# Remainders of the values formed on GpSimd, and a second tile of outputs, in an attention and expert kernel

## The chip, the cores and the metric

The kernel runs on one core of a Trainium2 chip. The metric is the device time of one execution in microseconds, as the median of several runs. Profiles come from one further execution, with every instruction's start and length on each engine.

## The reference

Attention with queries averaged in pairs, and then a mixture of experts in which each token goes to one expert:

```python
q_pool = q.reshape(B, H, S // 2, 2, D).mean(axis=3)          # B=8, H=8, S=1152, D=64
scores = scale * np.matmul(q_pool, k.transpose(0, 1, 3, 2))
attn = softmax(scores)                                       # 576 x 1152 for each head
x = np.matmul(attn, v)            # -> 4608 tokens of 512
logits = x @ w_gate + modality_bias[modality_id]
e_idx = np.argmax(logits, axis=1)
...
h = np.maximum(x[mask] @ w1[e], 0.0)                         # 8 experts, 512 -> 1024 -> 512
out[mask] = gate_w[mask, None] * (h @ w2[e])
```

All of it is in float32. The kernel multiplies in float16 and keeps the precision by splitting an operand x into a rounded part (hi) and the remainder x - hi (lo), and multiplying both.

## The kernel before

**Pairs.** One head of two batch elements makes a pair: their 64 columns each fill the 128 partitions. There are 32 pairs, and each has 18 steps in a loop. Two pairs next to each other are two heads of the same batch elements; their outputs go into one tile x2 (128 x 9 x 128 float32), each pair into one half of its columns.

**What is done for one pair.** `load_kq` and `load_v` fetch rawq, rawk and rawv. The queries are summed in pairs (L613), rounded (qh, L620), and their remainder is formed (lo, L648); the keys are rounded on ScalarE (hi, L632) and their remainders formed on GpSimd (lo, L648). qh goes by DMA into QB (L583), with which `maxpass` computes rounded scores on TensorE (L781) and VectorE takes the maximum of each row (L782). The row of maxima (mr, L766) is sent by DMA into the row B2 of operands (B<-mr, L767), and qh, hi and lo are sent into the operands B1 and B2 by `place`. Then `scores` multiplies (L843 and, with the row of maxima as one of its operands, L844), ScalarE takes the exponential (Pe, L845), and the lower halves of the exponentials are scaled into Pl on ScalarE (L826) and VectorE (L828). `pv` multiplies them by the values (L894 to L896).

**The values.** `square` (ScalarE, L694) finds their size; it uses the tile vl for its unneeded output. `power` and `scales` (TensorE, VectorE L706 and L708) make a power of two of it, sc. `values` then makes the rounded values VH = v * sc, in two parts of 640 and 512 columns (nine chunks of 128, five and four), and the remainders vl = v * sc - VH. From the third pair on, VH is made on GpSimd (L735) and vl on VectorE, in one instruction that scales and subtracts (L733). The first two pairs use other lines (L730, L731, L737). `shifted` makes a scaled copy VS of VH on VectorE (L745). VH and VS have three tiles, used in turn; rawv has two, vl three.

**Outputs.** When a head's value products are finished, `evac` divides them by the row sums and writes them into x2 on VectorE (L912, L913, L917): for the pair's first head (j = 0) and, some nine steps later, for its second (j = 1). After the second head of an odd pair the whole x2 is stored to the tensor xs in DRAM (L218). Five steps later `split_x` splits x2 into two float16 tiles (ScalarE L862, VectorE L869), and after an odd pair each is transposed by a DMA (L877) for the router's logits. There is one tile x2; the next pair's first `evac` writes into it once the store has read it.

**What sets the order.** On TensorE, ScalarE, VectorE and GpSimd the instructions run in the order in which the program gives them; each piece of work has a step, counted from the pair's first step, in constants (T_VH = -14 and -15 for the two parts of VH, T_VS = -12, T_VL = -11 and -2 for vl, T_QH = -26 for qh, T_LO for the lo). The DMAs are issued from SyncE's queue, in an order that isn't written out: the framework's scheduler chooses it, by its own estimate of when each one's data are ready. SyncE issues in that order and waits at each DMA for its data.

**Beside it.** The router's work is spread over the pairs' steps: logits, the routing of each group of tokens (`route`, small instructions on VectorE and GpSimd), and in the last pairs the lists of tokens for each expert (`first_list`). The router's set-up is done on GpSimd at step 25. After the attention the expert stage streams weights and runs until the end.

Of the kernel before, what the change touches and what calls it, by code (L numbers as in the profile page):

```python
# [9 lines left out]
F32 = mybir.dt.float32  # L10
# [6 lines left out]
ALU = mybir.AluOpType  # L17
# [5 lines left out]
P = 128  # L23
# [6 lines left out]
D = 64  # L30
# [49 lines left out]
QH_POOL = True  # L80
LO_POOL = (0, 1, 2)
VH_POOL = (0, 1)
EV_ACT = ()
IN_PM = (0, 1, 2, 3, 4, 5)
EVD = 1
# [10 lines left out]
NT = 9  # L96
# [452 lines left out]
def attention(tc, ctx, att, ident, npairs, xpool, on_two, on_split, on_scale, jobs, side, set_pm, started, ahead, hip):  # L549
# [3 lines left out]
    nc = tc.nc  # L553
# [25 lines left out]
    def need(p, *names):  # L579
        assert all((p, n) in made for n in names), f"pair {p}: {names} are not made yet"  # L580
# [137 lines left out]
    flat = lambda a: a.rearrange("p c j d -> p (c j) d")  # L718

    def values(p, i, lo):  # L720

        s = st[p]
        c = slice(*PARTS[lo][i:i + 2])
        made.add((p, f"v{'hl'[lo]}{i}"))
        if lo:
            need(p, f"vh{i}")
        v = flat(s["v"].rearrange("p (c j d) -> p c j d", c=NKC, j=2)[:, c])
        vh = flat(VH[p % 3][:, c, :, 0:D])
        if lo and p < 2:
            nc.gpsimd.tensor_scalar(v, v, s["sc"], None, op0=ALU.mult)  # L730
            nc.gpsimd.tensor_tensor(flat(s["vl"][:, c]), v, vh, op=ALU.subtract)  # L731
        elif lo:
            nc.vector.scalar_tensor_tensor(flat(s["vl"][:, c]), v, s["sc"], vh, op0=ALU.mult, op1=ALU.subtract)  # L733
        elif p > 1 and i in VH_POOL:
            nc.gpsimd.tensor_scalar(vh, v, s["sc"], None, op0=ALU.mult)  # L735
        else:
            nc.scalar.activation(vh, v, AF.Copy, scale=s["sc"])  # L737
# [117 lines left out]
    def split_x(p, x2):  # L855

        s = st[p]
        if p % 2 == 0:
            s["x"] = [xpool.tile([P, NT, 2 * D], F16, name=f"x{i}", bufs=1) for i in range(2)]
        hs = slice((p % 2) * D, (p % 2 + 1) * D)  # L860
        xh, xl = st[p - p % 2]["x"]
        nc.scalar.activation(xh[:, :, hs], x2[:, :, hs], AF.Copy, scale=s["sc"])  # L862
        later(XL, lambda: split_xl(p, x2))
# [16 lines left out]
    def pv(p, j, c):  # L880

        s = st[p]
        W = D + 2
        vh, vs, vl = VH[p % 3], VS[p % 3], s["vl"]
        need(p, "vs", f"vl{int(c >= PARTS[1][1])}")
        Ph, Pl, i = s["P", j, c // 3]
        x = D + (c % 3 if j else 2 - c % 3) * SQ
        if c == 0:
            s["xp"] = ps_pv.tile([P, 512], F32, name="xp", tag="pv")[:, 0:5 * W].rearrange("p (g w) -> p g w", w=W)
        xp = s["xp"]  # L890
        for g in range(5):
            o = x + g * P + (D if j and g < 4 else -D - 4 * P if j else 0)
            qs, out = slice(o, o + P), xp[:, g, 0:D + 1]
            nc.tensor.matmul(out, Ph[:, qs], vh[:, c, j, 0:D + 1], start=c == 0 and g == 0, stop=False, skip_group_check=True)  # L894
            nc.tensor.matmul(out[:, 0:D], Ph[:, qs], vl[:, c, j], start=False, stop=False, skip_group_check=True)  # L895
            nc.tensor.matmul(out, Pl[:, qs], vs[:, c, j, 0:D + 1], start=False, stop=c == NKC - 1, skip_group_check=True)  # L896
            if g == 4:
                free[i] -= 1
            if c == NKC - 1 and g == 4:
                later(0, lambda: evac(p, j, xp))  # L900
            yield

    def evac(p, j, xp):

        s = st[p]
        if p not in xts:
            xts[p] = xts[p - 1] if p % 2 else xpool.tile([P, NT, 2 * D], F32, name="x2")
        x2 = xts[p]
        hs = slice((p % 2) * D, (p % 2 + 1) * D)
        rs = sm.tile([P, 5], F32, name="rs")  # L910
        rr = sm.tile([P, 5], F32, name="rr")
        nc.vector.tensor_scalar(rs, xp[:, :, D], 1.0, EPS * PSC * LOW / 2 ** 16, op0=ALU.mult, op1=ALU.add)  # L912
        nc.vector.reciprocal(rr, rs)  # L913

        def part(r, g0, n, t0):
            m = r.stop - r.start
            nc.vector.scalar_tensor_tensor(x2[r, t0:t0 + n, hs], xp[r, g0:g0 + n, 0:D], s["isc"][r], rr[r, g0:g0 + n].unsqueeze(2).broadcast_to([m, n, D]),  # L917
                                           op0=ALU.mult, op1=ALU.mult)
        if j == 0:
            part(slice(0, P), 0, 5, 0)  # L920
        else:
            part(slice(0, P), 0, 4, 5)
            part(slice(D, P), 4, 1, 4)
            if p % 2:
                on_two(p // 2, x2)
            later(XD, lambda: split_x(p, x2))
# [6 lines left out]
    def later(n, fn):  # L933
        todo.setdefault(max(now[0] + n, flushed[0] + 1), []).append(fn)
# [25 lines left out]
    xts = {}  # L960
# [60 lines left out]
    for p in range(npairs):  # L1021
        b = NSTEP * p
        go = lambda t, f, *a, p=p, b=b, **k: at(b + t, p, lambda: f(p, *a), **k)
        if p > 1:
            d = D2 if p == 2 else (0,) * 5
            go(T_K2 - b if p == 2 else T_KQ, load_kq, end=False)
            go(T_SPLIT + d[0], split_q)
            go(T_QH + d[1], split_qh)
            for i in range(2):
                go(T_HI[i] + d[2], split_hi, i)  # L1030
            for i in range(3 if LOC else 7):
                go(T_LO[LOCI[i] if LOC else i] + d[3], split_lo, i)
            go(T_MAX + d[4], lambda p: mxq.append(maxpass(p)), end=False)
            go(T_PLACE + (T_P2 if p == 2 else 0), place, end=False)
            go(T_LV, load_v)
        elif p:
            go(T_P1 - b, place, end=False)
            go(T_M1 - b, lambda p: mxq.append(maxpass(p)), end=False)
            go(T_LV, load_v)
        sq, power_, vh, vs, vl = (T_SQ, T_POW, T_VH, T_VS, T_VL) if p > 1 else V1 if p else V0  # L1040
        if p == 1:
            go = lambda t, f, *a, p=p: at(t, p, lambda: f(p, *a))
        go(sq, square)
        go(power_, power)
        for i, t in enumerate(vh):
            go(t, values, i, False)
        go(vs, shifted)
        for i, t in enumerate(vl):
            go(t, values, i, True)
# [15 lines left out]
    for t in range(NSTEP * npairs):  # L1065
        p, c18 = divmod(t, NSTEP)
# [422 lines left out]
```

## Time and profile before

| | us |
|---|---|
| median of 3 runs | 1170.33 (1167.91 to 1176.4) |
| profiled execution | 1171.42 |
| its span, first to last instruction | 1169.70 |
| TensorE busy | 1113.4 |
| VectorE busy | 985.5 |
| ScalarE busy | 918.1 |
| GpSimd busy | 417.3 |

In the rows PE is TensorE (PEld its weight loads), DVE is VectorE, ACT is ScalarE, POOL is GpSimd and SPq is SyncE's queue. L733 is line 733 of the kernel. A group's row gives the line, engine and operation, the tile written and those read, shapes, the count, and then busy time in us, mean ns of one, and the idle time ahead of them with what ended it. A row of a timeline gives start and length in us, and in brackets the idle time ahead of the instruction with what ended it; equal instructions next to each other are merged. A row of waits gives who waited for whom, the total in us, the number of waits and the longest. The mean granted clock of TensorE is 0.996 of full speed.

### The profile page before, as it was taken

How to read it: one execution, taken by the hardware profiler on the slowest of the kernel's cores; microseconds unless marked ns; L12 is line 12 of the kernel's file. 1: busy time of each engine (PE TensorE's matmuls, PEld its weight loads, DVE VectorE, ACT ScalarE, POOL GpSimd, SP SyncE). 2: the span in 40 equal slices, each digit the busy share in tenths (PEclk: the TensorE clock that was granted, in tenths of full speed). 3: DMA queues.
4: the chain of work that ended last, by engine and by line, in shares of the span. 5: the costliest groups of instructions: out<-in, count | busy, mean ns of one | idle time of the engine just before them, and what ended most of it. 6: DMA issues, size and time to landing. Idle time of an engine off the chain costs nothing. (4 is left out here: it accounts for less than half of the span.)

```text
span 1169.7 us, 36628 instructions
## 1 busy us (share of the span) xinstructions
PE 1113.4 (95%) x14962; PEld 816.2 (70%) x14962; DVE 985.5 (84%) x2031; ACT 918.1 (78%) x1459; POOL 417.3 (36%) x393
## 2 busy tenths in 40 slices
PE   6989999999999999999999899999999999999995
PEld 2667777777777777777776677767667676676763
DVE  6898898999999999999999999888997757566661
ACT  5879999998999998999998888865466656566561
POOL 7743444444435344443444352123112121211200
PEclk9999999999999999999999999999999999999998
DMA  7667768767668678578577463499999999999970
GB/s 226 168 160 174 162 169 200 156 168 177 169 165 189 176 165 177 160 172 193 151 183 173 135 135 93 146 292 279 222 283 283 333 270 284 276 284 275 258 250 22
DMA packets 175569, 232.66 MB, mean 199 GB/s; under 512 B 92351, under 2 KB 126799, under 8 KB 175392
## 3 DMA queue, kind: packets, MB, share of 16 engines
q1 hardware_dynamic: 169254, 210.45, 69.4%
q0 software_dynamic: 6128, 19.78, 6.3%
q8 instruction: 119, 1.95, 0.7%
q14 instruction: 58, 0.48, 0.2%
q10 hardware_dynamic: 10, 0.00, 0.0%
HBM read 146.11 MB, written 19.18 MB: 141 GB/s over the span
## 5 line engine op out<-in xcount | busy, mean ns | idle before, releaser
L845 ACT ACTIVATE Pe<-psc 128x432 int32<-128x432 f32 x768 | 381.5, 527 | 65.1 <-PE psc L844 54.3
L782 DVE TENSOR_REDUCE mp<-pm 128x1 f32<-128x512 f32 x566 | 369.8, 683 | 13.7 <-PE pm L781 8.2
L894 PE MATMUL xp<-VH,Pe 128*128 128x65 f16 x2880 | 373.2, 193 | 0.0
L896 PE MATMUL xp<-VS,Pl 128*128 128x65 f16 x2880 | 372.6, 193 | 0.4 <-DVE Pl L828 0.4
L895 PE MATMUL xp<-vl,Pe 128*128 128x64 f16 x2880 | 371.3, 192 | 0.0
L895 PEld LDWEIGHTS <-Pe 128*128 128x128 f16 x2880 | 267.6, 98 | 87.8
L894 PEld LDWEIGHTS <-Pe 128*128 128x128 f16 x2880 | 272.1, 98 | 57.1 <-issue 19.4
L844 PE MATMUL psc<-B 65*128 65x432 f16 (+2 forms) x1152 | 306.7, 289 | 1.9 <-DMA B<-mr 1.8
L843 PE MATMUL psc<-B 128*128 128x432 f16 (+2 forms) x1152 | 306.0, 288 | 1.7 <-ACT Pe L845 1.7
L896 PEld LDWEIGHTS <-Pl 128*128 128x128 f16 x2880 | 266.4, 97 | 0.6 <-DVE Pl L828 0.5
L781 PE MATMUL pm<-hi,QB 128*128 128x512 f16 x566 | 215.4, 383 | 17.6 <-DVE mp L782 13.6
L826 ACT ACTIVATE Pl<-Pe 128x1152 f16<-128x1152 uint16 x186 | 216.5, 1164 | 5.9
L735 POOL TENSOR_SCALAR VH<-rawv,sc 128x512 f16<-128x512 f32 (+1 forms) x60 | 103.7, 1739 | 185.4 <-PE xp L896 125.4
L648 POOL TENSOR_TENSOR lo<-rawk,hi 128x576 f16<-128x576 f32 (+1 forms) x68 | 90.2, 1329 | 182.1 <-ACT hi L632 142.2
L1228 PE MATMUL ph<-xpart,w1h 128*128 128x256 f16 x544 | 148.3, 273 | 0.1
L1230 PE MATMUL ph<-xpart,w1l 128*128 128x256 f16 x544 | 148.3, 273 | 0.0
L1229 PE MATMUL ph<-xpart,w1h 128*128 128x256 f16 x544 | 148.3, 273 | 0.0
L844 PEld LDWEIGHTS <-B 65*128 65x128 f16 x1152 | 113.4, 98 | 25.8 <-issue 3.2
L843 PEld LDWEIGHTS <-B 128*128 128x128 f16 x1152 | 113.0, 98 | 9.0 <-issue 3.7
L828 DVE TENSOR_SCALAR Pl<-Pe 128x576 f16<-128x576 uint16 (+1 forms) x198 | 108.1, 546 | 8.5 <-ACT Pe L845 7.1
L1276 PE MATMUL po<-w2h,hl 128*128 128x512 f16 x296 | 112.2, 379 | 0.0
L1275 PE MATMUL po<-w2l,hh 128*128 128x512 f16 x296 | 112.2, 379 | 0.0
(263 smaller groups left out, 1790.6 us busy)
## 6 DMA issues: line engine op xcount, KB each, us to landing
w2r<-in_w_dram SPq DMA_DIRECT2D x76, 512.0 KB
w1r<-in_w_dram SPq DMA_DIRECT2D x72, 512.0 KB
rawv<-in_att_dram SPq DMA_DIRECT2D x32, 576.0 KB
B<-hi SPq DMA_DIRECT2D x128, 144.0 KB
rawq<-in_att_dram SPq DMA_DIRECT2D x31, 576.0 KB
rawk<-in_att_dram SPq DMA_DIRECT2D x31, 576.0 KB
B<-qh SPq DMA_DIRECT2D x128, 72.0 KB
B<-lo SPq DMA_DIRECT2D x64, 144.0 KB
```

Of the source, the lines that this page charges most:

```text
L781: nc.tensor.matmul(pm, QB[p % 2][:, u], s["hi"][:, t * 512:(t + 1) * 512], start=True, stop=True)
L782: nc.vector.tensor_reduce(mp[:, u, t:t + 1], pm, op=ALU.max, axis=AX.X)
L826: nc.scalar.activation(low, rest, AF.Copy, scale=LOW)
L843: nc.tensor.matmul(o, b1[:, ks], b1[:, qs], start=True, stop=False, skip_group_check=True)
L844: nc.tensor.matmul(o, b2[:, ks], b2[:, qs], start=False, stop=True, skip_group_check=True)
L845: nc.scalar.activation(Pe[:, D + x0:D + x1], pt, AF.Exp, scale=1.0 / 16)
L894: nc.tensor.matmul(out, Ph[:, qs], vh[:, c, j, 0:D + 1], start=c == 0 and g == 0, stop=False, skip_group_check=True)
L895: nc.tensor.matmul(out[:, 0:D], Ph[:, qs], vl[:, c, j], start=False, stop=False, skip_group_check=True)
L896: nc.tensor.matmul(out, Pl[:, qs], vs[:, c, j, 0:D + 1], start=False, stop=c == NKC - 1, skip_group_check=True)
L1228: nc.tensor.matmul(o, hi[:, c, fs], xh[:, :, c], start=c == 0, stop=False)
L1229: nc.tensor.matmul(o, hi[:, c, fs], xl[:, :, c], start=False, stop=False)
L1230: nc.tensor.matmul(o, lo[:, c, fs], xh[:, :, c], start=False, stop=c == 3)
```

## The change

From the third pair on (p >= 2), GpSimd multiplies the part of rawv by sc in place, copies it into VH (which rounds it to float16), and later subtracts VH from rawv into vl; the steps of these stay as they were. VectorE's instruction for vl is no longer used, nor is GpSimd's old line for VH. The tile x2 gets two buffers, so that two pairs after the next use another one than those before.

```diff
+VLP = 2
...
         vh = flat(VH[p % 3][:, c, :, 0:D])
-        if lo and p < 2:
+        if p >= VLP:
+            if lo:
+                nc.gpsimd.tensor_tensor(flat(s["vl"][:, c]), v, vh, op=ALU.subtract)
+            else:
+                nc.gpsimd.tensor_scalar(v, v, s["sc"], None, op0=ALU.mult)
+                nc.gpsimd.tensor_copy(vh, v)
+        elif lo and p < 2:
             nc.gpsimd.tensor_scalar(v, v, s["sc"], None, op0=ALU.mult)
             nc.gpsimd.tensor_tensor(flat(s["vl"][:, c]), v, vh, op=ALU.subtract)
...
         if p not in xts:
-            xts[p] = xts[p - 1] if p % 2 else xpool.tile([P, NT, 2 * D], F32, name="x2")
+            xts[p] = xts[p - 1] if p % 2 else xpool.tile([P, NT, 2 * D], F32, name="x2", bufs=2)
```

## The prediction

> **What bounds the kernel now.** I read the busy times of the page first, then busy time cut at the pairs (each window runs from one pair's squaring on ScalarE to the next one's), then the groups of instructions, the waits, and the timelines of GpSimd, SyncE's queue and VectorE in one pair. The chain that ended last covers only the tail of the expert stage, which the change doesn't touch; what counts is the attention stage, the first two thirds of the span.
>
> ```profile
> PE 1113.4 (95%) x14962; PEld 816.2 (70%) x14962; DVE 985.5 (84%) x2031; ACT 918.1 (78%) x1459; POOL 417.3 (36%) x393
> ...
> 213.30:234.90 21.60, 21.60 (x372) 16.80 (x370) 19.60 (x44) 20.79 (x37) 9.56 (x7) 1.00 0.88 181
> 257.40:281.60 24.20, 22.36 (x382) 17.11 (x380) 23.43 (x60) 21.41 (x39) 10.22 (x9) 1.00 0.79 171
> 437.40:461.60 24.20, 22.36 (x382) 17.11 (x381) 23.43 (x61) 21.42 (x38) 10.21 (x9) 1.00 0.81 162
> 618.20:643.00 24.80, 22.34 (x381) 17.08 (x380) 24.08 (x67) 21.62 (x39) 10.44 (x9) 1.00 0.74 171
> 643.00:668.80 25.80, 23.35 (x398) 17.68 (x395) 25.34 (x63) 21.69 (x37) 9.81 (x7) 1.00 0.48 140
> 668.80:693.80 25.00, 22.41 (x372) 16.96 (x370) 24.43 (x65) 21.64 (x37) 10.49 (x7) 1.00 0.68 133
> 693.80:718.20 24.40, 23.25 (x391) 17.56 (x390) 24.01 (x59) 21.61 (x36) 7.94 (x6) 1.00 0.35 87
> 718.20:742.60 24.40, 22.84 (x412) 17.96 (x411) 23.18 (x64) 21.20 (x37) 3.62 (x3) 1.00 0.50 126
> ```
>
> After each window come its length, the busy time of PE, PEld, DVE, ACT and POOL, the granted clock and the DMA share. In a plain pair (213.30) TensorE is busy for all of its 21.60 us: VectorE at 19.60 isn't the limit, and taking work from it there brings nothing. In seven pairs that carry routing or listing besides, VectorE is busy 95 to 98% and TensorE idle: 1.84, 1.84, 2.46, 2.45, 2.59, 1.15 and 1.56 us, 13.9 us together. Only there does the moved work pay directly. So I price the change by what TensorE gets back in the pairs where it idles, not by the time that VectorE is spared.
>
> **The change: what leaves VectorE, what GpSimd gets.**
>
> ```profile
> L733 DVE SCALAR_TENSOR_TENSOR vl<-rawv,sc,VH 128x640 f16<-128x640 f32 (+1 forms) x60 | 50.6, 844 | 0.0
> ...
> L735 POOL TENSOR_SCALAR VH<-rawv,sc 128x512 f16<-128x512 f32 (+1 forms) x60 | 103.7, 1739 | 185.4 <-PE xp L896 125.4 <-PE psc L844 30.3 <-PE pm L781 19.1
> ...
> L620 POOL CAST qh<-rawq 128x576 f16<-128x576 f32 x30 | 20.1, 670 | 0.1
> ...
> L730 POOL TENSOR_SCALAR rawv<-rawv,sc 128x640 f32<-128x640 f32 (+1 forms) x4 | 7.4, 1850 | 7.7 <-ACT VH L737 4.5 <-issue 3.2
> L731 POOL TENSOR_TENSOR vl<-rawv,VH 128x640 f16<-128x640 f32 (+1 forms) x4 | 5.2, 1288 | 0.3
> ```
>
> Removed: 60 VectorE instructions of 0.844 us, 1.69 us in each of 30 pairs. On GpSimd the scaling stays, now in place (1.74 becomes at most 1.85), and each pair gains two casts (0.670 for 576 columns, so 1.34 for 1152) and two subtractions of 1.29: 3.92 us on top of 9.56. GpSimd is then busy 13.5 of 21.6 us, so it isn't the bound. New waits: the in-place scaling must come after ScalarE's squaring of the same tile, but its scale is made from that squaring, so it already does. The value products on TensorE now wait for GpSimd's remainders instead of VectorE's; they belong to the next pair and start a dozen us later, so nothing queues there. The next load into rawv waits for the second subtraction on GpSimd instead of one on VectorE; both are over long before its place in SyncE's queue. No engine gets an instruction whose wait holds up others, except GpSimd itself, and that is a matter of order.
>
> **Order matters on GpSimd.** Its queue has, in a plain pair:
>
> ```profile
> 216.46 3.43 POOL L735 TENSOR_SCALAR VH<-rawv,sc 128x512 f16<-128x512 f32 x2 [5.67 <-PE xp L896]
> 219.83 0.67 POOL L620 CAST qh<-rawq 128x576 f16<-128x576 f32 x1
> 220.59 1.28 POOL L648 TENSOR_TENSOR lo<-rawq,qh 128x576 f16<-128x576 f32 x1
> 224.55 1.59 POOL L648 TENSOR_TENSOR lo<-rawk,hi 128x576 f16<-128x576 f32 x1 [2.68 <-ACT hi L632]
> ...
> 223.15 0.46 DVE L745 TENSOR_SCALAR VS<-VH 128x1152 f16<-128x1152 f16 x1
> ```
>
> Both casts (1.34) and, by the steps in the code, the first subtraction (640 columns, about 1.43) come before qh. So VH is ready at about 221.2 instead of 219.89; its reader VS starts on VectorE at 223.15, so that costs nothing, but with 1.9 us of cover only. qh comes 2.77 us later; the idle 2.68 us before the lo of k takes that up, and everything from 224.55 on stays in place. The second subtraction falls into the idle time after the last lo. The cost of the 3.92 us on GpSimd's own side is therefore nothing as long as its idle time (2.68 us ahead of the lo, 5.67 ahead of VH) covers it. What is late is qh alone, and SyncE's queue waits for it, since QB<-qh is the first DMA behind it.
>
> **SyncE's queue, and the tile of outputs.**
>
> ```profile
> 216.50 2.53 SPq L583 DMA_DIRECT2D B<-hi  x4
> 220.53 1.10 SPq L583 DMA_DIRECT2D QB<-qh  x2
> ...
> 222.85 1.28 SPq L218 DMA_DIRECT2D xs<-x  x1
> 224.22 1.44 SPq L583 DMA_DIRECT2D B<-qh  x1
> 226.46 4.43 SPq L877 DMA_TRANSPOSE xt<-x  x2
> 230.99 0.79 SPq L767 DMA_DIRECT2D B<-mr  x1
> ...
> 234.80 0.35 PE L844 MATMUL psc<-B 65*128 65x432 f16 x1
> ```
>
> In every second pair the row of maxima (B<-mr) is issued behind two transposes, and the next pair's first L844 needs it, 3.81 us later here. How much room that leaves shows another pair:
>
> ```profile
> 592.29 0.79 SPq L767 DMA_DIRECT2D B<-mr  x1
> ...
> 595.92 0.34 PE L844 MATMUL psc<-B 65*128 65x432 f16 x1 [0.39 <-DMA B<-mr]
> ...
> DVE x L917 <- DMA xs<-x: 18.5, 9, 2.9
> ...
> 123.30:145.40 22.10, 21.57 (x371) 16.71 (x370) 19.47 (x44) 21.00 (x38) 9.56 (x7) 1.00 0.85 179
> ...
> 573.10:595.20 22.10, 21.42 (x371) 16.56 (x369) 19.32 (x44) 20.86 (x37) 9.56 (x7) 1.00 0.84 170
> ```
>
> There TensorE waits, 3.63 us after the issue: the room in the pair before is about 0.2 us (3.81 - 3.63). So the second buffer's 18.5 us of VectorE waits aren't 18.5 us of time. They lie in nine of these pairs, and seven of them (the first and last are shown) have 4.6 us of idle TensorE in all; when VectorE no longer stands still, the row of maxima ends the pair at almost the same moment. The gain is between 0 and 4.6 us; both ends are as near, so I take half, 2.3.
>
> Is qh's delay passed on? The queue stands idle from 225.66 (224.22 + 1.44) to 226.46, 0.80 us; in the old order a delay of 2.77 puts the transposes and the row 1.97 us later. But the order on SyncE isn't written by hand, and in the pair from 257.40, where a routing step holds qh back, it is another one:
>
> ```profile
> 267.25 0.38 SPq L218 DMA_DIRECT2D xs<-x  x1
> 270.60 1.11 SPq L583 DMA_DIRECT2D QB<-qh  x2
> ...
> 273.07 4.07 SPq L877 DMA_TRANSPOSE xt<-x  x2
> 277.24 0.79 SPq L767 DMA_DIRECT2D B<-mr  x1
> ```
>
> The store xs goes ahead of QB there, and the transposes aren't late. I take it that the planner does this in the other pairs too: cost 0, with 1.97 us for each such pair as the other end (first rival).
>
> **The shared access of VectorE and GpSimd.**
>
> ```profile
> 218.16 0.95 DVE L828 TENSOR_SCALAR Pl<-Pe 128x576 f16<-128x576 uint16 x1
> 222.78 0.46 DVE L828 TENSOR_SCALAR Pl<-Pe 128x576 f16<-128x576 uint16 x1
> ...
> 89.92 1.22 DVE L828 TENSOR_SCALAR Pl<-Pe 128x576 f16<-128x576 uint16 x1 [1.97 <-ACT Pe L845]
> ...
> 89.54 1.28 POOL L648 TENSOR_TENSOR lo<-rawk,hi 128x576 f16<-128x576 f32 x1 [3.61 <-ACT hi L632]
> ```
>
> L828 takes 0.46 us alone, 0.95 beside GpSimd's scaling, 1.22 beside its subtraction. A pair has eight such instructions (six L828, VS, L869); 3.92 us more of GpSimd in 21.6 makes 8 x 3.92 / 21.6 = 1.45 more meetings. At 0.49 to 0.76 us each, with GpSimd as the loser in about half (the lo at 224.55 took 1.59 instead of 1.28), that is 0.45 us a pair; the ends are 0 and 1.1.
>
> [...]
>
> **Sum.** Seven late pairs: 1.69 - 0.45 = 1.24 us each, 1.15 where TensorE idles no longer than that: 8.6 us gained. Buffer: 2.3 gained. The start costs something:
>
> ```profile
> 67.94 0.39 PE L781 MATMUL pm<-hi,QB 128*128 128x512 f16 x1 [1.18 <-DMA QB<-qh]
> ```
>
> TensorE waits here for QB already, so the third pair's casts and subtraction ahead of qh cost up to their 2.77 us (0 to 2.8; I take 2.8). In the code the router's set-up stands between that pair's scaling and qh as well, so GpSimd has no idle time there that would take the delay up. If it did, the term would be 0. Together 8.1 us less. The profiled execution took 1171.42 us (span 1169.70 and 1.72 around it), so 1163.3; it lies 1.1 above the median of 1170.33, so against the median **1162**.
>
> **Rivals.** *SyncE keeps its order* (slower). Every second pair then waits for the row of maxima. From 1.0 us of delay to qh (0.80 idle and 0.2 room) it decides; at 2.77 nine plain pairs lose 1.8 us each, 16 us, the buffer's 2.3 go, and half of the late pairs' 8.6: 1171.4 + 16 + 2.8 - 4.3 = 1186, on the median 1185. For it: the queue already waits for qh from 219.03 (216.50 + 2.53) to 220.53, 1.5 us in which it could have sent something else, so the planner takes qh to be earlier than it is; against it: the pair at 267.25. Chance 0.24. *Everything comes back*: xs moves ahead of QB, lands sooner, the transposes behind it, which take 4.43 us to issue now, go faster, and TensorE's idle 13.9 + 4.6 us all go, the start costing nothing: 1152.9, or 1152. Against it: 1.69 us of relief can't fill idle times of up to 2.59, so it needs the order of the queue to help in the late pairs too. Chance 0.18. *Nothing moves*, because the relief isn't one: meetings at 1.1 us leave 0.6 of 1.69, 4 us in seven pairs, and the start takes 2.8 back, 1169. Chance 0.13. The forecast has 0.45, with a range of its own from 1156 (meetings at 0, the start at 0) to 1168 (meetings at 1.1, some of the queue's delay).
>
> One per cent, 11.7 us, is about what a measurement tells from no change: below 1158.6 lie most of the second rival and a quarter of the forecast, 0.27; above 1182 most of the first, 0.21; between them 0.52. The range goes from 1151 to 1187, so as to hold the ends of both rivals.
>
> **What would show it.** Right: no L733 group; L917 without waits for xs; xs issued ahead of QB in plain pairs; pairs from 618 on 1.2 us shorter, plain ones within 0.3 of 21.6. Wrong: waits of L844 for B<-mr in every second pair (SyncE), VS waiting for VH on GpSimd (the 1.9 us of cover gone), or L828's mean far above 0.6 us (meetings).

## The result: 1188 us, 1.2% slower, and the profile after

The changed kernel takes 1188.01 us (median of 6 runs, 1181.03 to 1192.75) against 1171.13 for the kernel before on the same chip: ratio 1.0124, 95% interval 1.0093 to 1.0155. The profiled execution took 1189.69 (span 1188.0). The forecast of 1162 was wrong in its sign; 1188 lies 1 us beyond the range, next to the price of the slower rival (1185). In the changed kernel the lines have moved: L694, L620, L648, L583, L218 are L695, L621, L649, L584, L219; L745, L767, L781, L782, L790, L828, L843 to L845 and L877 are 7 higher. New are L732 (subtraction), L734 (scaling in place) and L735 (cast).

The busy times of the page after:

```profile
PE 1117.1 (94%) x14962; PEld 819.3 (69%) x14962; DVE 983.0 (83%) x1971; ACT 917.1 (77%) x1459; POOL 535.4 (45%) x513
```

GpSimd has 118 us more, VectorE hardly less: 50.6 us of remainders left it, and 31 of them came back in two groups alone (shown further down). Busy time at intervals from one squaring to the next after the change (length, then PE, PEld, DVE, ACT, POOL, granted clock, DMA share, GB/s):

```profile
210.00:232.00 22.00, 21.81 (x371) 16.71 (x370) 20.43 (x44) 20.93 (x38) 13.69 (x11) 1.00 0.78 165
232.00:256.80 24.80, 22.30 (x393) 17.35 (x393) 21.17 (x48) 21.28 (x36) 15.13 (x16) 1.00 0.66 165
370.40:396.60 26.20, 24.07 (x394) 18.57 (x394) 21.34 (x45) 21.43 (x37) 13.31 (x11) 0.93 0.59 160
511.00:537.70 26.70, 24.08 (x394) 18.39 (x393) 21.62 (x45) 21.33 (x36) 13.52 (x11) 0.94 0.59 155
605.30:632.50 27.20, 23.90 (x393) 18.23 (x392) 21.11 (x48) 21.29 (x36) 15.16 (x16) 0.94 0.66 152
682.40:711.10 28.70, 24.95 (x372) 18.77 (x371) 25.91 (x59) 21.47 (x38) 13.52 (x11) 0.88 0.52 131
```

The first row is the same interval as 213.30 before (21.60), 0.4 longer. The second is the one behind it; its kind was about 22.5 before. In the other four the granted clock is below 1, which it was in no interval of before.

To see where the 18.6 us lie I added up the distances between the starts of the squarings (L694, L695) of each trace: the start (to the fourth interval), the twelve even plain intervals (4, 6, ... 26), the nine odd plain ones, and the six with routing or listing (11, 19, 27 to 30; an interval has the number of its pair, counted from 0). Behind the last squaring no kernel differs by more than 2 us from the kernel before.

| us | start | 12 even | 9 odd | 6 late | last squaring |
|---|---|---|---|---|---|
| before | 101.1 | 270.5 | 198.3 | 148.4 | 718.2 |
| after | 97.7 | 289.6 | 197.5 | 152.0 | 736.8 |
| x2_only | 101.2 | 275.1 | 194.6 | 148.2 | 719.0 |
| vl_only | 97.2 | 271.0 | 211.4 | 152.2 | 731.9 |
| before_qh_first | 97.3 | 267.7 | 194.6 | 149.5 | 709.2 |
| after_xs_act | 99.8 | 265.9 | 202.0 | 152.2 | 719.9 |
| before_x2_xs_act2 | 100.8 | 268.9 | 194.6 | 148.6 | 712.9 |
| after_xs_act2 | 99.9 | 266.0 | 197.5 | 153.3 | 716.7 |
| after_to29_xs_act2 | 98.4 | 266.5 | 197.5 | 146.4 | 708.8 |
| before_qh_late | 109.6 | 284.6 | 215.2 | 158.9 | 768.3 |

The change loses 19.1 us in the even intervals and 3.6 in the late ones, and gains 3.4 at the start and 0.8 in the odd ones. From the waits after (total us, times, longest):

```profile
PE psc L851 <- DMA B<-mr: 17.1, 11, 3.3
```

The waits of VectorE for xs are gone, as they should be. In their place TensorE waits for the row of maxima. SyncE's queue after, at the same place as shown of before:

```profile
220.59 1.10 SPq L584 DMA_DIRECT2D QB<-qh  x2
...
222.48 0.40 SPq L219 DMA_DIRECT2D xs<-x  x1
...
223.62 5.96 SPq L884 DMA_TRANSPOSE xt<-x  x2
229.67 0.79 SPq L774 DMA_DIRECT2D B<-mr  x1
...
232.73 0.38 SPq L604 DMA_DIRECT2D rawv<-in_att_dram  x1
```

Counted from the interval's squaring (213.30 before, 210.00 after), QB goes from 7.23 to 10.59 us, the store xs from 9.55 to 12.48, the transposes only from 13.16 to 13.62, but they take 5.96 instead of 4.43 to issue, and the row of maxima goes from 17.69 to 19.67: 2.0 later. The order was planned anew, but not as I took it: xs stays behind QB, and what moved back is the load of rawv. The store, 9 x 128 x 128 floats, is now issued 1.14 us ahead of the transposes (before 3.61).

The interval shown of before is the earliest of its nine odd plain ones. Over all nine the row of maxima is issued 17.7 to 19.3 us behind the squaring before (18.6 in the mean) and 19.3 to 20.0 after (19.7), so it is 1.1 us later in the mean; the two transposes take 4.4 to 6.0 us before and 5.5 to 6.2 after. Before, TensorE waits for the row in three of the nine, 0.2 to 0.4 us; after, in each of them, 0.9 to 3.3 us.

### The profile page after: what moved, and what is told of

Read it like the earlier page. It is cut to its first block, busy times and chain, and to the rows that moved or that the text cites. A ratio compares the mean times of both kernels' runs of the same rounds, so it can differ in the third digit from the quotient of the medians.

```text
span 1188.0 us, 36750 instructions
## 1 busy us (share of the span) xinstructions
PE 1117.1 (94%) x14962; PEld 819.3 (69%) x14962; DVE 983.0 (83%) x1971; ACT 917.1 (77%) x1459; POOL 535.4 (45%) x513
## 5 line engine op out<-in xcount | busy, mean ns | idle before, releaser
L851 PE MATMUL psc<-B 65*128 65x432 f16 (+2 forms) x1152 | 308.1, 290 | 18.1 <-DMA B<-mr 17.1
L734 POOL TENSOR_SCALAR rawv<-rawv,sc 128x512 f32<-128x512 f32 (+1 forms) x60 | 108.1, 1802 | 156.0 <-PE psc L851 55.2
L649 POOL TENSOR_TENSOR lo<-rawk,hi 128x576 f16<-128x576 f32 (+1 forms) x68 | 84.1, 1239 | 120.5 <-ACT hi L633 83.5
L835 DVE TENSOR_SCALAR Pl<-Pe 128x576 f16<-128x576 uint16 (+1 forms) x198 | 124.4, 629 | 9.1 <-ACT Pe L852 7.7
L1292 POOL DMA_INDIRECT out_dram<-o,siB x25 | 27.8, 1113 | 203.4 <-ACT o L1289 166.9
```

The source lines that it names most:

```text
L851: nc.tensor.matmul(o, b2[:, ks], b2[:, qs], start=False, stop=True, skip_group_check=True)
```

## The experiments

Each kernel was timed against the kernel before (1171.6 to 1172.5 in these comparisons); the ratio has its 95% interval. Three questions: which half of the change costs, by which way, and what the moved work costs by itself.

### Each half alone

**x2_only**: the kernel before with the second tile.

```diff
-            xts[p] = xts[p - 1] if p % 2 else xpool.tile([P, NT, 2 * D], F32, name="x2")
+            xts[p] = xts[p - 1] if p % 2 else xpool.tile([P, NT, 2 * D], F32, name="x2", bufs=2)
```

> Before, with the second buffer of x2 alone; the order on SyncE is the one of before. Theory 1 (the queue: in every second pair the row of maxima, behind the store xs and the transposes on SyncE, sets the end of the pair): the 18.5 us of VectorE waits for xs go, but the pairs that had them shorten by 0.3 us at most, and the next pair's first L844 waits instead; 1167 to 1171, with 2 to 5 us of waits of L844 for B<-mr. Theory 2 (VectorE is the limit there, and GpSimd's contention ate what the change gave): nine pairs gain what TensorE idled, 4 to 6 us: 1164 to 1166.

Measured: 1171.64, ratio 0.9993 (0.9970 to 1.0017). One row of its waits:

```profile
PE psc L844 <- DMA B<-mr: 8.5, 8, 1.6
```

VectorE's 18.5 us of waits for xs have vanished and the odd intervals are 3.7 us shorter, but TensorE's waits for B<-mr rise from 1.8 to 8.5 and the even intervals are 4.6 longer. The tile's gain is handed on to the row of maxima, whole: theory 1's mechanism, with more waits for the row than its 2 to 5 us and a time 0.6 us above its range.

**vl_only**: the changed kernel with one tile x2.

```diff
-            xts[p] = xts[p - 1] if p % 2 else xpool.tile([P, NT, 2 * D], F32, name="x2", bufs=2)
+            xts[p] = xts[p - 1] if p % 2 else xpool.tile([P, NT, 2 * D], F32, name="x2")
```

> The change without the second buffer of x2. Theory 1: qh comes as late as in the changed kernel, so the store xs is issued about 3 us later than before and x2 is free later; VectorE waits for xs 4 to 6 us in every second pair, ahead of the row of maxima's user, so 1188 to 1200. Theory 2: contention costs the same as in the changed kernel, and VectorE, relieved of L733, takes the old waits of about 2 us: 1188 to 1192.

Measured: 1188.46, ratio 1.0160 (1.0101 to 1.0220). Its waits:

```profile
DVE x L924 <- DMA xs<-x: 29.1, 10, 4.9
...
PE psc L851 <- DMA B<-mr: 1.5, 4, 0.5
```

The same time by another door: the late store now holds VectorE at the tile (29.1 us against 18.5; both theories allowed the time, these waits speak for theory 1), the odd intervals take the loss, and the row of maxima is nearly in time. So the moved work carries the whole loss, and the second tile only chooses where it is paid.

### qh earlier

**before_qh_first** and **after_qh_first**: GpSimd makes qh at the step T_SPLIT (-34; T_QH is -26), ahead of the values, in the kernel before and in the changed one.

```diff
-            go(T_QH + d[1], split_qh)
+            go(T_QH + d[1] if p == 2 else T_SPLIT, split_qh)
```

> Before, with qh moved in the same way. Theory 1: SyncE no longer stands 1.5 us for qh in the plain pairs, xs goes out earlier, the transposes are farther behind it and the row of maxima is earlier; odd pairs lose their L844 waits and part of the xs waits: 1163 to 1169. Theory 2: nothing but GpSimd's order changes, 1169 to 1172.

> The changed kernel with qh rounded straight behind the sum of the queries (step -34 instead of -26), ahead of VH and the remainders on GpSimd; nothing else is changed, and GpSimd has as much to do. Theory 1: QB no longer holds the queue, xs is issued within 2 us of its data and the row of maxima comes at least 1 us earlier against its making; waits of L844 fall from 17 us below 6, time 1164 to 1176. Theory 2: the meetings of VectorE and GpSimd stay (VS at 0.9, L828 at 0.63), so the time stays at 1183 to 1190.

Measured: 1163.82, ratio 0.9928 (0.9907 to 0.9949), and 1182.02, ratio 1.0085 (1.0056 to 1.0114). SyncE's queue in the first of them:

```profile
216.03 0.38 SPq L218 DMA_DIRECT2D xs<-x  x1
...
220.90 4.02 SPq L877 DMA_TRANSPOSE xt<-x  x2
225.01 0.80 SPq L767 DMA_DIRECT2D B<-mr  x1
```

The store goes 4.87 us ahead of the transposes, and the kernel *before* already gains 8 us: a part of this loss was there without the change. In the changed kernel QB is out of the way too, but there rawq, ahead of the store, waits for the remainder of the queries, which is late on GpSimd just as qh was; TensorE still waits 8.2 us for B<-mr. The time of after_qh_first lies between the ranges of its two theories.

**after_qhlo_first**, **before_qhlo_first**, **after_qhlo_vl_late**: that remainder is moved forward as well; in the third the values' subtraction is four steps later besides.

```diff
-                go(T_LO[LOCI[i] if LOC else i] + d[3], split_lo, i)
+                go(T_SPLIT if p > 2 and i == 0 else T_LO[LOCI[i] if LOC else i] + d[3], split_lo, i)
```

> The changed kernel with qh and the remainder of the queries (lo) both straight behind the sum of the queries, ahead of VH. With qh alone moved, SyncE's next load (rawq) still waited for that lo, and xs went out 3.6 us late. Theory 1 (queue) says xs now leaves within 0.6 us of its data and the waits of L844 for B<-mr fall from 8.2 to below 3 us. Theory 2 (contention) says that VS still meets the first subtraction: odd plain pairs stay at 22.5 instead of 21.6, TensorE idle 1 us before L781. Both act, so the time: 1174 to 1179; the queue alone would give 1155 to 1163, contention alone 1182.

> Before, with qh and that lo moved ahead of VH. Against qh alone (1163.8, ratio 0.993): by theory 1 rawq no longer holds the queue either, and the row of maxima comes up to 0.8 us earlier, so 1160 to 1164. If the queue is already free of qh with the first move, nothing more is gained: 1162 to 1165.

> As after_qhlo_first, and the first subtraction four steps later (-7 instead of -11), behind the lo of k, so that it no longer runs when VectorE makes VS; GpSimd's work is the same. If contention is a matter of which instructions meet, VS falls from about 0.93 us to below 0.6, odd plain pairs to 21.7, and the time lies 6 to 12 us below that of after_qhlo_first, 1160 to 1168. If it is a matter of how much GpSimd does, the meetings move to L828 and the time stays within 3 us.

Measured: 1178.69 (ratio 1.0050, 1.0028 to 1.0071), 1170.55 (0.9985, 0.9965 to 1.0005) and 1178.54 (1.0053, 1.0027 to 1.0078). The first met its time by neither of its two ways: the waits for the row are 15.8 us, not below 3, while VS falls to 453 ns on average and the odd intervals to 21.62. The third's time is the first's, as its second theory said; its profiled execution (1171.4) is far from its median and isn't read here. The second is a plain miss: of the 8 us that early qh alone had brought, the early remainder takes 7 back; its late intervals sum to 154.1 us (148.4 before). The order of a queue that nobody writes out answered each shift on GpSimd with another one, so this way couldn't settle the mechanism.

### The store on another queue

**after_xs_act** and **before_xs_act**: the store alone is issued from ScalarE's queue; **before_x2_xs_act** has the second tile too.

```diff
-            rt.store(g, cc, x2, eng)
+            rt.store(g, cc, x2, nc.scalar if eng is nc.sync else eng)
```

> The changed kernel with the store xs issued from ScalarE's queue instead of SyncE's. It goes out when its data are there, not behind qh; ScalarE pays some 0.4 to 1.3 us for it in every second pair. If the store's 576 KB, issued 1.2 us ahead of the transposes, is what makes them and the row of maxima late, the first transpose takes below 2.5 us (3.5 now), L844's waits fall from 17 below 8 us, and the time is 1176 to 1182. If the late qh acts in another way (QB, rawq, the place of rawv), it stays at 1185 to 1190.

> The kernel before with one edit: the store of the outputs (xs) is issued from ScalarE's queue instead of SyncE's. Theory queue (what costs is that the store, held up in SyncE's queue by QB's wait, is issued just ahead of the transposes, which then run behind its data): in the kernel before the store is issued 1.4 to 1.9 us after its data in plain pairs and the transposes take 2.8 + 2.0 us, so part of the cost is there already: the intervals that end with a row of maxima lose 0.5 us each or more, the waits for the single tile x2 go down, 1163 (1156 to 1168). Rival (SyncE's place costs only once the change has delayed it, since the kernel before had the room): 1169 to 1172.

> The kernel before with the store from ScalarE's queue and two tiles x2, that is, the changed kernel with the same store but the remainders left on VectorE. Against the changed kernel with that store (1169.8) it gives the price of the moved work by itself. Theory queue with contention (meetings on GpSimd's and VectorE's shared access cost about 1 us a pair, and idle TensorE is only partly saved): 1158 (1153 to 1164), 6 to 17 us below the changed kernel. Rival (the moved work is free once the store is out of the way, and relieves the late pairs as predicted): 1169 to 1176, no better than the changed kernel.

Measured: after_xs_act 1169.83, ratio 0.9981 (0.9962 to 0.9999): one edit gives the change's loss back, by more than its theory's 1176 to 1182. before_xs_act 1171.53 (0.9999, 0.9980 to 1.0018), before_x2_xs_act 1172.23 (0.9996, 0.9978 to 1.0015): no gain, against the theory. What eats it stands in the waits of after_xs_act:

```profile
PE psc L850 <- ACT Pe L852: 12.3, 20, 1.7
...
PE psc L851 <- DMA B<-mr: 1.0, 1, 1.0
```

The row of maxima is on time (17.1 us of waits have become 1.0), but ScalarE waits at the store for the last outputs, with the exponentials behind it, some 1 us in every odd interval; in before_xs_act TensorE waits for the exponentials in the same way, 13.5 us (1.7 before). **before_qh_first_x2_xs_act** has early qh on top.

> The kernel before with three edits: qh made first on GpSimd (at the step of the split, T_SPLIT), two tiles x2, the store from ScalarE's queue. Theory queue: no plain pair has anything left to wait for, odd intervals 21.6, even ones 22.1; 1155 (1151 to 1161), the fastest of all. Rival (early qh and the store's queue are two ways to the same gain): as before_qh_first, 1162 to 1165.

Measured: 1170.82, ratio 0.9992 (0.9976 to 1.0008), a miss for the same reason: its odd intervals sum to 204.1.

So the next three issue the store two steps later, behind three more exponentials:

```diff
-            rt.store(g, cc, x2, eng)
+            if eng is nc.gpsimd:
+                rt.store(g, cc, x2, eng)
+            else:
+                later(2, lambda: rt.store(g, cc, x2, nc.scalar))
```

> The changed kernel with the store issued from ScalarE's queue two steps later than in after_xs_act, behind three more exponentials, so that ScalarE has no wait at it. Theory (the moved work costs nothing in plain pairs, the loss was the store's place): plain pairs 21.7 and 22.15, B<-mr never waited for, 1160 (1156 to 1165). Rival (meetings of GpSimd and VectorE cost about 1 us a pair once ScalarE's wait no longer covers them): odd intervals stay near 22.4, 1168 to 1172.

> The same store and two tiles x2, the remainders on VectorE as in the kernel before. Theory (ScalarE's wait of 1.07 us at the store was the only cost of before_x2_xs_act): plain pairs 21.62 and 22.15, 1161 (1157 to 1165); the difference to after_xs_act2 is the price of the moved work, within 4 us. Rival (the moved work costs by itself): 1155 to 1161 here, and 8 us or more below after_xs_act2.

> As before_x2_xs_act2, and qh made first on GpSimd. Theory (early qh, the store's place and the tile all act on the same waits, and these are gone with the store alone): 1158 to 1163, no better than before_x2_xs_act2. Rival (early qh brings something of its own, as the 8 us of before_qh_first): 1150 to 1156.

Measured: 1165.89 (0.9946, 0.9930 to 0.9962), 1166.42 (0.9954, 0.9939 to 0.9969) and 1164.98 (0.9946, 0.9931 to 0.9962), each 1 to 2 us above the range of its theory. SyncE's queue in the first, the changed kernel, whose interval begins at 210.1:

```profile
220.65 1.10 SPq L584 DMA_DIRECT2D QB<-qh  x2
...
223.60 3.52 SPq L884 DMA_TRANSPOSE xt<-x  x2
227.22 0.79 SPq L774 DMA_DIRECT2D B<-mr  x1
```

and ScalarE's queue has the store earlier:

```profile
218.40 0.37 ACTq L219 DMA_DIRECT2D xs<-x  x1
```

QB is as late as in the change (220.59), the transposes start as they did (223.62), yet they take 3.52 us instead of 5.96 (3.5 to 4.0 over the nine odd plain intervals, where the change has 5.5 to 6.2), and the row of maxima goes out 2.45 earlier. Only the store is missing ahead of them. This tells "the store just ahead of them makes the transposes slow" from "everything behind QB is late". And with the store gone the moved work costs nothing on balance: 1165.89 against 1166.42. By the table it loses 2.9 us in the odd intervals and 4.7 in the late ones, and gains 2.9 in the even ones and 0.9 at the start. The even ones gain, as I read it, since the change's order sends rawv's load behind the row of maxima; in before_x2_xs_act2 that load, 576 KB too, goes ahead of the transposes, they take 4.0 to 5.6 us, and TensorE waits 3.1 us for the row (0.9 in after_xs_act2). No run moved that load alone.

### The delay alone

**before_qh_late** and **before_qh_late2**: the kernel before with five or two fills ahead of qh, of a tile that nobody reads.

```diff
+        if p > 2:
+            pause = sm.tile([P, 576], F16, name="pause", bufs=1)
+            for _ in range(5):
+                nc.gpsimd.memset(pause, 0.0)
```

> The kernel before with five fills of 128x576 float16 on GpSimd ahead of qh, into a tile that nobody reads, some 2.8 us in all from the third pair on: the delay that the change gives qh, without its work. Theory queue: QB is late by about as much, the store xs behind it too, the transposes take 3 us and more for the first, B<-mr lands late and L844 waits for it in most second pairs; with one x2 the waits for xs grow as well: 1183 (1177 to 1192), even though VectorE's L828 keeps its mean near 0.54 us. Rival (the loss comes from the meetings of GpSimd and VectorE): fills read nothing and meet little, 1171 to 1175.

> The kernel before with two fills of 0.62 us on GpSimd ahead of qh instead of five: 1.25 us of delay. By the prediction's rival the cost begins at 1.0 us of delay: 1172 to 1176. Theory (the store is then issued nearer the transposes at once, and a wait for xs or B<-mr grows from the first tenth of a microsecond): about two fifths of before_qh_late's 48 us without its half-clock stretches, some 15 us: 1185 (1178 to 1192).

Measured: 1220.51, ratio 1.0407 (1.0366 to 1.0448), and 1170.74, ratio 0.9981 (0.9963 to 0.9999). In both the kernel before's lines behind the edit are 4 higher (L881 is L877). Groups, SyncE's queue and one row of the waits of the first (the interval begins at 225.9):

```profile
L832 DVE TENSOR_SCALAR Pl<-Pe 128x576 f16<-128x576 uint16 (+1 forms) x198 | 109.1, 552 | 7.7 <-ACT Pe L849 6.3
L749 DVE TENSOR_SCALAR VS<-VH 128x1152 f16<-128x1152 f16 x31 | 26.8, 864 | 1.2 <-ACT VH L741 1.2
L622 POOL MEMSET pause<- 128x576 f16 x145 | 84.1, 580 | 6.7
```

```profile
236.40 1.22 SPq L583 DMA_DIRECT2D QB<-qh  x2
...
238.35 0.41 SPq L218 DMA_DIRECT2D xs<-x  x1
...
239.50 5.98 SPq L881 DMA_TRANSPOSE xt<-x  x2
245.58 0.79 SPq L771 DMA_DIRECT2D B<-mr  x1
```

```profile
DVE x L921 <- DMA xs<-x: 28.7, 10, 5.7
```

From the squaring these are 10.50, 12.45, 13.60 and 19.68 us; the change has 10.59, 12.48, 13.62 and 19.67. A delay of 2.9 us without any of the change's work rebuilds its timetable on SyncE to a tenth of a microsecond, while L828's mean stays at 552 ns. The run isn't free of meetings, though: VS takes 864 ns (459 before), and at 235.78 it takes 0.91 us beside the late rounding of qh (0.88 us from 235.50), as in the change. That it costs 48 us, beyond the theory's range, isn't the queue's doing alone: with one tile VectorE waits 28.7 us for xs, the start loses 8.5, and the mean granted clock falls to 0.977. TensorE's waits for the row, which the theory expected in most second pairs, are 3.3 us in all, as few as with one tile in vl_only (1.5). With two fills (1.16 us) the queue in a plain interval, from 351.2, is

```profile
357.57 0.53 SPq L603 DMA_DIRECT2D rawv<-in_att_dram  x1
359.62 1.10 SPq L583 DMA_DIRECT2D QB<-qh  x2
...
364.54 4.66 SPq L881 DMA_TRANSPOSE xt<-x  x2
369.30 0.80 SPq L771 DMA_DIRECT2D B<-mr  x1
```

with B<-mr at 18.1 us behind its squaring (17.1 to 18.5 over the nine, 17.8 in the mean, 0.8 earlier than before), and no loss. QB is 1.16 us later, but the order was planned anew here as well: the load of rawv now fills the wait ahead of QB. My theory of a cost from the first tenth (1185) fell; the prediction's rival, with a cost from 1.0 us of delay, is the nearer one. Both delayed kernels have this order, so between them only the delay differs: the cost sets in somewhere between 1.2 and 2.9 us.

### The late pairs

**after_to29_xs_act2**: as after_xs_act2, but the last three pairs make their values as before.

```diff
-        if p >= VLP:
+        if VLP <= p < 29:
```

> As after_xs_act2, but the last three pairs keep the kernel before's way of making their values (the remainders on VectorE). Theory (in the pairs with listing the moved work ends in VectorE waiting beside GpSimd's subtractions, and then in half-clock stretches): the intervals of pairs 29 and 30 go back from 28.3 and 27.3 us to 25.3 and 24.4, 1160 (1157 to 1163). Rival (these two pairs lose it to something else in the order of the work): they stay above 27, 1165 to 1167.

Measured: **1160.96**, ratio 0.9900 (0.9871 to 0.9929), the fastest of all kernels here. The intervals of pairs 29 and 30, first in after_xs_act2, then in this one:

```profile
661.10:689.40 28.30, 24.56 (x372) 18.59 (x370) 25.62 (x59) 21.36 (x38) 13.52 (x11) 0.88 0.52 127
689.40:716.70 27.30, 24.35 (x395) 18.50 (x393) 25.55 (x59) 21.47 (x37) 12.23 (x10) 0.94 0.25 64
```

```profile
660.00:684.40 24.40, 22.27 (x372) 16.93 (x370) 23.87 (x62) 21.50 (x38) 10.14 (x7) 1.00 0.53 131
684.40:708.80 24.40, 23.25 (x391) 17.55 (x390) 24.01 (x58) 21.59 (x37) 7.94 (x6) 1.00 0.34 87
```

6.8 us came back in two intervals, and the clock is whole. What had happened there can be seen in the changed kernel in pair 29, first on VectorE's timeline, then on GpSimd's:

```profile
694.20 1.54 DVE L752 TENSOR_SCALAR VS<-VH 128x1152 f16<-128x1152 f16 x1
695.65 1.62 DVE L482 TENSOR_TENSOR ol<-lof,lane 128x384 bf16<-128x384 f32 x1
```

```profile
693.93 1.48 POOL L649 TENSOR_TENSOR lo<-rawq,qh 128x576 f16<-128x576 f32 x1
695.38 1.48 POOL L649 TENSOR_TENSOR lo<-rawk,hi 128x576 f16<-128x576 f32 x1
```

VS and the listing's L482, which take 0.46 and 0.55 us in before_x2_xs_act2, each end 0.3 to 0.4 us behind the end of the GpSimd subtraction that they started beside. These two subtractions are old work that the new work makes late. before_qh_late, which only makes them late, has L482's counterpart busy for 13.7 us in all, as the changed kernel has with 1.62 us in both pairs (before 12.5), and the intervals at 28.6 and 27.9. VS alone isn't enough: in pair 28 of the changed kernel it takes 1.54 us too, and that interval loses nothing (25.5 against 25.8). With the moved work TensorE waits up to 3.2 us for VectorE's maxima in these two intervals, and without it up to 1.0; that the meetings make these waits is argued from the rows.

**after_to29_qh_first_xs_act2**: early qh besides.

> The same with qh made first on GpSimd. Theory (nothing in plain pairs waits for qh any more): 1160, the same as after_to29_xs_act2 within 2 us, ahead of before_qh_first's 1163.8. Rival (early qh brings something of its own): 1153 to 1157.

Measured: 1176.45, ratio 1.0022 (1.0002 to 1.0042), missed by both theories. Its group of VS:

```profile
L752 DVE TENSOR_SCALAR VS<-VH 128x1152 f16<-128x1152 f16 x31 | 38.0, 1226 | 1.2 <-ACT VH L744 1.2
```

Without early qh it has 820 ns. VS takes 0.46 us alone and 1.54 beside a subtraction, so I estimate from the 1226 that with early qh a subtraction stands beside it in most pairs; TensorE waits 16.9 us for VectorE's maxima (10.0 without early qh). That this is the cause of all 15 us is argued from these rows; no run moved VS alone. Other runs fit: the odd plain intervals take 21.62 us on average where VS takes 453 ns (after_qhlo_first), 21.95 at 894 (after_xs_act2) and 22.9 at the 1226 here.

## Why the prediction was wrong

**The bound and the parts** held. The scaling in place took 1802 ns (at most 1.85 was said), the casts 668 (670), the subtractions 1238 (1290); GpSimd is busy 13.69 us in a plain pair (13.5), qh comes 3.1 us later against the squaring (2.77), and VS doesn't wait for VH on GpSimd. First two groups of before, then those after:

```profile
L828 DVE TENSOR_SCALAR Pl<-Pe 128x576 f16<-128x576 uint16 (+1 forms) x198 | 108.1, 546 | 8.5 <-ACT Pe L845 7.1
L745 DVE TENSOR_SCALAR VS<-VH 128x1152 f16<-128x1152 f16 x31 | 14.2, 459 | 1.2 <-ACT VH L737 1.2
...
L835 DVE TENSOR_SCALAR Pl<-Pe 128x576 f16<-128x576 uint16 (+1 forms) x198 | 124.4, 629 | 9.1 <-ACT Pe L852 7.7
L734 POOL TENSOR_SCALAR rawv<-rawv,sc 128x512 f32<-128x512 f32 (+1 forms) x60 | 108.1, 1802 | 156.0 <-PE psc L851 55.2 <-PE xp L903 46.6 <-PE pm L788 15.4
L732 POOL TENSOR_TENSOR vl<-rawv,VH 128x640 f16<-128x640 f32 (+1 forms) x60 | 74.3, 1238 | 2.5
...
L752 DVE TENSOR_SCALAR VS<-VH 128x1152 f16<-128x1152 f16 x31 | 29.0, 934 | 1.2 <-ACT VH L744 1.2
```

**The step that failed** is the one under SyncE's queue: "I take it that the planner does this in the other pairs too: cost 0". One pair with another order, in which routing held qh back, was read as what the planner would do for any delay. The planner, which is the framework's scheduler, kept xs behind QB. The other end of that step, 1.97 us later for B<-mr, came as 2.0 in the interval that had been read and as 1.1 in the mean of the nine; the reason beside it was half right, since in that interval the transposes start only 0.46 later and take 1.53 longer, behind the store. So the first rival came (1185), with its place, its row and nearly its time. Its chance of 0.24 was too low: the idle 1.5 us in the queue, which I put down in its favour, was a look at this planner's habit in *every* plain pair, and weighed more than the one at 267.25.

**The rival's price** was 1.8 us for nine pairs, 16; TensorE's waits for the row rose by 15.3 (1.8 to 17.1), and the even intervals lost 19.1. That the price fits is partly luck: the row was late by less than said, but in the other eight plain pairs of before it had less room than in the one read, and in two after it was used only 4.8 and 5.3 us behind its issue. Of the 19.1, 5.1 us are no waits at all but the clock: 26.20 x 0.07 + 26.70 x 0.06 + 27.20 x 0.06. The fourth interval, 28.70 x 0.12 = 3.4, is nearly the whole loss of the late ones. 8.5 of 18.6 us lie there.

**The relief of the late pairs**, 8.6, was mis-sized. Where the moved work did no harm (intervals 11, 19, 27 and 28 of after_to29_xs_act2 against before_x2_xs_act2: 23.85, 23.87, 24.36, 25.51 against 24.16, 24.16, 24.75, 25.82) it is 0.33 us a pair, not 1.24; in the two with listing it was a loss. **The meetings**, put at 0.45 us a pair, are on VectorE (124.4 - 108.1 + 29.0 - 14.2) / 30 = 1.04, near the end of 1.1 that I had given: VS, 459 ns before and 934 after, meets nearly always, since order, not chance, decides who meets whom: in plain pairs the late rounding of qh stands beside it (0.89 us from 219.68; VS takes 0.92 us from 219.97). The shared access that I named no run shows as such; the runs show how long the two engines' instructions take side by side. With the store out of the way the odd intervals are 0.33 us longer (21.95 against 21.62), 2.9 in all, and I put that down to VS.

**The tile** brought 0 of the 2.3 taken, an end of its range, and by the mechanism named for it. **The start** gained 3.4 instead of losing 2.8: TensorE waits 0.5 us for QB there (1.2 before), so qh's delay didn't arrive; before_qh_first, without the moved work, gains as much (97.3). Which relief pays there wasn't tried.

## What to carry to other kernels

Of work that is moved to an idle engine, follow the *next* thing that engine owes, here qh, to the queue that waits for it, and ask which transfer will then stand directly ahead of an urgent one; 1.2 us of delay cost nothing here, with an order planned anew around it, and 2.9 cost 48. An order that a planner made is not to be taken over from one odd case: where the plain pairs show it waiting, count on its waiting longer, and read all of them, since the one read here had the most room. And before an engine's relief is booked as time, see which of its instructions will now stand beside the new ones: the fastest kernel here keeps the moved work in the plain pairs, leaves it out where lists are made, and sends the store by another queue.

## What the runs showed of the hardware

**Half the clock behind a wait of 2.0 us.** The stretch after the wait at 370, in windows of 1 us:

```profile
370.00:371.00 1.00, 0.37 (x5) 0.12 (x4) 0.69 (x1) 1.00 (x3) 0.00 (x0) 1.00 0.08 10
371.00:372.00 1.00, 0.00 (x0) 0.00 (x0) 0.00 (x0) 0.60 (x2) 0.00 (x0) 1.00 0.97 199
372.00:373.00 1.00, 0.65 (x8) 0.45 (x8) 0.00 (x0) 0.27 (x1) 0.00 (x0) 1.00 1.15 184
373.00:374.00 1.00, 1.00 (x14) 0.81 (x12) 0.96 (x2) 0.73 (x2) 0.00 (x0) 0.56 0.83 258
374.00:375.00 1.00, 1.00 (x7) 0.62 (x6) 0.10 (x1) 0.32 (x2) 0.00 (x0) 0.50 1.01 387
375.00:376.00 1.00, 1.00 (x21) 1.00 (x20) 0.83 (x2) 0.97 (x2) 0.00 (x0) 0.50 0.99 364
376.00:377.00 1.00, 1.00 (x16) 0.71 (x14) 0.34 (x5) 0.58 (x2) 0.64 (x1) 0.73 1.05 312
```

TensorE idles for 2.0 us, and then the granted clock is at a half for some 3.4 us (0.44 + 0.50 + 0.50 + 0.27 = 1.7 us lost): the wait and the stretch together cost nearly twice the wait's length. Another wait, 2.5 us in the interval from 232.00, leaves the clock whole:

```profile
234.50 0.34 PE L851 MATMUL psc<-B 65*128 65x432 f16 x1 [2.52 <-DMA B<-mr]
```

Of the changed kernel's nine waits for the row behind odd plain intervals, the half clock came behind those of 1.9, 2.0 and 3.3 us, and not behind this one or the five of 0.9 to 1.6 us. No run shows what decides it.

**A transpose behind a store.** A pair of DMA transposes takes 5.5 to 6.2 us to issue, over nine intervals, when it goes 1.1 to 1.2 us behind a store of 576 KB on the same queue (the changed kernel), and 3.5 to 4.0 (3.52 at 223.60) with that store on another queue 5.2 us or more earlier (at 218.40; after_xs_act2). Queue and distance changed together there. The distance alone doesn't decide: 3.6 us behind the store on the same queue the kernel before has 4.43 us at 226.46 and 5.95 at 586.25. The row of maxima behind the transposes was used 4.83 us after its issue (229.67 to 234.50) where TensorE waited for it, against 3.63 before (592.29 to 595.92); over the nine waits after it is 3.4 to 5.3.
